# Sums over neighbours by accumulating DMAs in a two-attention kernel on one Trainium2 core

## The chip, the cores and the metric

The kernel runs on one core of one Trainium2 chip. The metric is the device time of one execution in microseconds (us); the time before is the median of three runs. The engines are TensorE (PE), VectorE (DVE), ScalarE (ACT), GpSimd (POOL) and SyncE (SP). In the kernel before, SP starts every DMA.

## What is computed

One sequence of 2048 positions with 512 features goes through two attentions with 32 heads of width 16. A is full attention. B is local: each position looks at itself and at seven earlier ones, two apart. A gate per position mixes the two results.

```python
x = A_x                                              # (1, 2048, 512) bf16
g = _sigmoid((x * gate_w).sum(-1, keepdims=True))
# A: full attention, H = 32, Dh = 16
scores = jnp.einsum("bhqd,bhkd->bhqk", q, k) * (Dh ** -0.5)
o = jnp.einsum("bhqk,bhkd->bhqd", _softmax(scores, axis=-1), v)
a = o.transpose(0, 2, 1, 3).reshape(B, S, D) @ A_wo
# B: local attention, W = 8 neighbours, dil = 2
idx = pos[:, None] - (jnp.arange(W) * dil)[None, :]  # masked where idx < 0
logits = jnp.einsum("bhsd,bhswd->bhsw", q, kg) * scale
o = jnp.einsum("bhsw,bhswd->bhsd", _softmax(logits, axis=-1), vg)
b = o.transpose(0, 2, 1, 3).reshape(B, S, D) @ B_wo
return g * a + (1 - g) * b
```

In both attentions q, k and v are `x @ wqkv`. The change touches the last sum of B, over the eight neighbours w of attn[w] * vg[w].

## The kernel before

**Full attention (A).** The queries are split into four chunks of 512 positions, and the heads into eight groups of four. A chunk with a group is a period; there are 32. In each period the scores of 16 key tiles for four heads are made by PE in two PSUM rings of three and two banks. ACT turns each ring into exponentials (`pT`), 683 such instructions in the whole kernel, and PE multiplies them with v into the one bank `acc`. A part of the exponentials (3 to 12 tiles a period) is made by DVE with integer arithmetic instead: `dt_a` or `wkv` from the bank `D`, then three shifted copies `pd_a`. At the end of a period DVE transposes `acc` (`accT`), POOL scales it by the denominators and the gate (`rden`, `ott`), and DVE transposes every second one into `oat`, which holds the transposed results of one chunk and comes in two buffers (`po3`, L1241).

**Local attention (B).** It runs beside A, 16 tiles of 128 positions (`b_tile`, L799). PE projects k, v and q of the tile into the one PSUM bank `misc_ps`, DVE copies them to `kvs` and `qb`, and SP writes `kvs` to the DRAM scratch `kv_scr`. From there SP loads the shifted keys and values, four neighbours in each of two loads (`ksh`, `vsh`, 512 KB each, in three shared buffers `gat`). The rest is done by POOL in pieces of 128x256:

- the logits: 16 products `prod<-ksh,qb` and their additions into `lg` (about 22 us),
- the softmax: `sm_sub` on POOL after a maximum by DVE, the exponential on ACT, sums and reciprocals on DVE, then the gate (`sm_gate`) and `sm_mul` on POOL,
- the weighted values: 16 products `prod<-vsh,lg` (`av_mul`, L920) and 14 additions (`av_add`, L936), which add neighbours pairwise in `prod` and into `ob`, the last two into the bf16 tile `obb`.

The pieces of logits and values of one tile are strung together by `chain_ops` (L948). The result `obb` is transposed by PE into `misc_ps` (`fin`, L1006) and copied by DVE to `obt`, which holds the four tiles of a chunk and comes in two buffers.

**Output projections.** When a chunk of A is complete (the last `oat` is written) and B's tile is in `obt`, PE multiplies both with the two output weights into one bank, eight matmuls a tile, two at a time (`ab_part`, L1275). DVE copies the sum to `osb` and SP stores it. In the last chunk a part of this is left for the very end.

**The order.** Nothing is ordered by hand. Every step is an `Op` with an engine, an assumed duration, a due time (`dl`), the steps it needs, and tokens for the buffers that it allocates and uses. `list_schedule` (L159) plays these steps on a model of the five engines and writes one fixed order for every engine, into which the program is then emitted. On the chip every engine goes through its list in that order and waits at semaphores. The starts of B's tiles are given: the first at 36, then 44 to 49 apart (`b_space`), each allowed to start its projections 70 earlier. Due times of B's steps are offsets from these starts. The due times of the output projections are offsets from the end of A's chunk, `E`, which is the sum of assumed durations of A (L1273):

```python
dl = E + (4.0 + 4.0 * tt if last else 10.0 + 14.0 * tt)
```

A step on POOL is assumed to last `PRE` plus a price per element by its kind:

```python
NS = dict(bb=0.00189, bf=0.00178, ff=0.00212, one=0.0011)
GP = lambda kind, n: [(False, PRE), (True, NS[kind] * n)]
```

Of the kernel before, what the change touches and what calls it, by code (L numbers as in the profile page):

```python
# [8 lines left out]
ACT = mybir.ActivationFunctionType  # L9
ALU = mybir.AluOpType  # L10
AX = mybir.AxisListType
FP32 = mybir.dt.float32
# [17 lines left out]
W = 8  # L30
# [35 lines left out]
class Op:  # L66

    def __init__(self, eng, occ, fn, dl, deps=(), alloc=(), use=(), lat=None, rel=0.0, name="",
                 mode="f", js=(), full=0.0, fill=False, scores=None, after=(), ride=False, parts=None):
        self.scores, self.ride, self.parts = scores, ride, parts  # L70
# [16 lines left out]
NS = dict(bb=0.00189, bf=0.00178, ff=0.00212, one=0.0011)  # L87
GFIRST = -300.0
PRE = 0.14
GP = lambda kind, n: [(False, PRE), (True, NS[kind] * n)]  # L90
# [68 lines left out]
def list_schedule(ops, zeros):  # L159
# [16 lines left out]
    def avail(o):  # L176
        t = o.ready
        for tk in o.alloc:
            r = tk.res
            n = len(r.order)  # L180
            if n >= r.cap:
                for u in r.order[n - r.cap].ops:
                    if u.done is None:
                        return INF
                    t = max(t, u.end + SELF[u.eng] if u.eng == o.eng else u.done)
        return t
# [15 lines left out]
    while len(out) < len(ops):  # L202
# [54 lines left out]
        for s_ in succ.get(o, ()):  # L257
            left[s_] -= 1
            if left[s_] == 0:
                s_.ready = max([s_.rel] + [d.end + SELF[d.eng] if d.eng == s_.eng else d.done for d in s_.deps] + [d.t for d in s_.after])  # L260
                cand[s_.eng].append(s_)
# [4 lines left out]
def kernel(  # L266
# [156 lines left out]
    kv_scr = tc.dram_tile([16 + S, 2 * D], BF16, name="kv_scr")  # L423
    NH = NG // 2
    woarr = const.tile([128, NH, D], BF16, name="woarr")
    ident = const.tile([128, 128], BF16, name="ident")
    identf = const.tile([128, 128], FP32, name="identf")
    rowc = const.tile([128, 3], FP32, name="rowc")
# [23 lines left out]
    omg = const.tile([128, NT], FP32, name="omg")  # L452
    e1 = const.tile([128, NT], FP32, name="e1")
    d1 = const.tile([128, NT], FP32, name="d1")

# [23 lines left out]
    def init_pool2():  # L479
        make_identity(nc, identf[:])  # L480
        G.memset(vp_all[:, 0, :, :], 1.0)
        G.memset(vp_all[:, 1:NT, :, DH:DH + 1], 1.0)
# [283 lines left out]
    def zsig():  # L766
        A.activation(out=e1[:], in_=st_g["zp"][:, 0:NT], func=ACT.Exp, scale=-1.0)

    def zgate():
        V.tensor_scalar_add(out=d1[:], in0=e1[:], scalar1=1.0)  # L770
        V.reciprocal(out=g_sp[:], in_=d1[:])
        V.tensor_tensor(out=omg[:], in0=e1[:], in1=g_sp[:], op=ALU.mult)

    def zrows():
        st_g["zr"] = misc_ps([128, NT, TPC])
        for s_ in range(TPC):
            for j in range(4):
                mm(st_g["zr"][32 * j:32 * j + 32, :, s_], identf[:, 32 * s_:32 * s_ + 32], g_sp[:], True, True,
                   tile_position=(0, 32 * j))
# [14 lines left out]
    obt_tiles, obt_tok = {}, {}  # L794
    WH = W // 2
    WP = WH // 2
    HB = D // 2

    def b_tile(t):  # L799
# [52 lines left out]
        tks, tvs = [tok("gat", NGA), tok("gat", NGA)], [tok("gat", NGA), tok("gat", NGA)]  # L852
        tlg, tob, tbb = tok("lg", 2), tok("ob", 1), tok("obb", 1)
        kvd_ = o_kvd[max(0, t - 1):t + 1] + [o_zr]
# [3 lines left out]
        def logits_mul(hf, wp, w_, c0):  # L858
            def s():
                if hf == 0 and wp == 0 and w_ == 0 and c0 == 0:  # L860
                    st["lg"] = work.tile([128, H, W], FP32, name="lg", tag="lg", bufs=2)
                if w_ == 0 and c0 == 0:
                    st["prod", hf, wp] = work.tile([128, WP, D], FP32, name="prod", tag="prod", bufs=2)
# [56 lines left out]
        def av_mul(hf, wp, w_, c0):  # L920
            def s():
                if wp == 0 and w_ == 0 and c0 == 0:
                    key = ("ob", "obb")[hf]
                    st[key] = work.tile([128, D], (FP32, BF16)[hf], name=key, tag=key, bufs=1)
                if w_ == 0 and c0 == 0:
                    st["prod", hf, wp] = work.tile([128, WP, D], FP32, name="prod", tag="prod", bufs=2)
# [4 lines left out]
                G.tensor_tensor(out=st["prod", hf, wp][:, w_, c0:c0 + HB].rearrange("p (h d) -> p h d", d=DH),  # L931
                                in0=st["vsh", hf][:, wp + w_, c0:c0 + HB].rearrange("p (h d) -> p h d", d=DH),
                                in1=attn_bc, op=ALU.mult)
            return s, "bf", HB
# [12 lines left out]

        def chain_ops(seq, dls, alloc, toks):  # L948

            made, tps, a, seen = {}, {}, None, set()  # L950
            for n_, (g_, k_, (f, kind, n), src, deps) in enumerate(seq):
                new = g_ not in tps
                if new:
                    tps[g_] = tok("prod", 2)
                al, us = list(alloc.get((g_, k_), ())), []
# [27 lines left out]
        aseq = []  # L983
        loads["k", t], loads["v", t] = lk, lv
# [7 lines left out]
        a = op("pool", 0.0, sm_mul, GFIRST, deps=[a], use=[tlg], parts=GP("ff", H * W))  # L992
        for g_, (hf, wp) in enumerate(halves):
            k1 = range(1 if not hf and not wp else 2)
            ps_ = mulp(av_mul, hf, wp) + [av_add(hf, wp, c0, k_) for k_ in k1 for c0 in range(0, D, HB)]
            srcs = [None] * nm + [2, 3] + [nm, nm + 1]
            gs_ = [(g_, k_, p_, srcs[k_], ([lv[hf], a] if k_ == 0 else [])) for k_, p_ in enumerate(ps_)]
            aseq += [gs_[k_] for k_ in (0, 2, 4, 1, 3, 5, 6, 7) if k_ < len(gs_)]
        a1 = chain_ops(aseq, tb + 40, {(0, 0): [tob], (WH // WP, 0): [tbb]},
                       lambda g_: [tlg, tvs[g_ // (WH // WP)], tob] + ([tbb] if g_ >= WH // WP else []))  # L1000
        a1.lat += SM_LAT[3]
        tk = tok("misc", 1)
        if cb not in obt_tok:
            obt_tok[cb] = tok("obt", 2)

        def fin():  # L1006
            if cb not in obt_tiles:
                obt_tiles[cb] = work.tile([128, DC, QW], BF16, name="obt", tag="obt", bufs=2)
            st["ptp"] = misc_ps([128, DC, 128], BF16)
# [202 lines left out]
    for pi, (c_, i) in enumerate(periods):  # L1212
        st = {}
        if i == 0:
            oat_tok[c_] = tok("oat", 2)
        if i % 2 == 0:
# [24 lines left out]
        def po3(pi=pi, c_=c_, i=i):  # L1241
            if c_ not in oat_tiles:
                oat_tiles[c_] = work.tile([128, NH, QW], BF16, name="oat", tag="oat", bufs=2)
            V.transpose(out=oat_tiles[c_][:, i // 2, :], in_=ott2[:, (pi // 2) % 2].rearrange("p b d -> p (b d)"))
# [21 lines left out]
    for t in range(NT):  # L1266
# [5 lines left out]
        E = S0[NG * c_ + ng]  # L1272
        dl = E + (4.0 + 4.0 * tt if last else 10.0 + 14.0 * tt)  # L1273

# [95 lines left out]
```

## Time and profile before

| | |
|---|---|
| median of three runs | 825.94 us (825.35 to 826.28) |
| profiled execution, its own time | 826.04 us |
| its span in the profile | 824.3 us |
| mean granted TensorE clock | 0.994 |
| DMA | 47.37 MB, 57 GB/s on average |
| DMAs started by POOL | none |

The span runs from the first to the last instruction of the program; the 1.74 us between it and the execution's own time lie around it. Busy time of an engine is the time in which one of its instructions ran; a matmul's end is modelled. In the waits a line reads: engine, what it writes, what it waited for, then the total in us, the number of waits and the longest. In the groups by form a line reads: line of the code, engine, operation, output and inputs with their shapes, the count, then the busy us, the mean ns of one, and the idle time ahead of them. In the timeline a line begins with its start and its length in us, and ends with the idle time of the engine ahead of it and what ended that. L323 and L332 are helpers through which nearly all instructions are issued, so the tiles' names tell them apart. L1011 is `fin`.

### The profile page before, as it was taken

What the parts mean: (1) busy time and instruction counts of PE and PEld (TensorE: products, weight loads), DVE (VectorE), ACT (ScalarE), POOL (GpSimd) and SP (SyncE); (2) the same over time, 40 slices, a digit from 0 to 9 for tenths busy, and PEclk for the clock granted to TensorE, in tenths of its full rate; (3) what the DMA queues carried; (4) which work ended last, traced back from release to release, by engine and by line L of the source; (5) the groups of instructions that cost most, each with busy time, mean ns of one, the idle gap of its engine ahead of it and who ended that gap; (6) DMA issues with size and microseconds to landing.
All of it is one profiled execution on the core that took longest, in us unless ns stands there. A gap on an engine that the chain in (4) does not pass through costs nothing.

```text
span 824.3 us, 18657 instructions
## 1 busy us (share of the span) xinstructions
PE 777.9 (94%) x7314; PEld 247.4 (30%) x7358; DVE 706.3 (86%) x1111; ACT 785.9 (95%) x706; POOL 720.4 (87%) x1196
## 2 busy tenths in 40 slices
PE   7999999999999999999999999999999999999996
PEld 4333433333322222222222222222222222222231
DVE  5456876788978999989999899999989899998987
ACT  3899999999899899999999999999999999999995
POOL 5097999999999999899999999899999999899960
PEclk9899999999999999999999999999999999999999
DMA  9203020112111220211112111211111211110000
GB/s 296 78 3 116 2 90 28 65 52 65 57 48 65 65 66 28 63 53 47 63 35 77 57 50 51 65 53 49 43 52 54 82 34 65 52 52 27 27 1 26
DMA packets 44440, 47.37 MB, mean 57 GB/s; under 512 B 2352, under 2 KB 41776, under 8 KB 44352
## 3 DMA queue, kind: packets, MB, share of 16 engines
q1 hardware_dynamic: 44352, 46.18, 17.6%
q8 instruction: 57, 0.93, 0.5%
q14 instruction: 31, 0.25, 0.1%
HBM read 39.85 MB, written 6.32 MB: 56 GB/s over the span
## 4 chain that ended last, share of the span: by engine, by line
ACT 47%; PE 31%; issue 18%; DVE 2%; DMA 1%; SPq 0%; DVEq 0%; ACTq 0%
ACT pT L323 46%; PE acc L332 11%; PE ring L332 9%; PE misc_ps L332 8%; PE D L332 3%; DMA xld<-in_A_x_dram 1%; ACT lg L323 1%; DVE pd_a L323 0%; DVE kt_all L323 0%; PE pxt L584 0%; PE misc_ps L1011 0%; DVE dt_a L323 0%; DVE qt L323 0%; DVE vp_all L323 0%; DVE wkv L323 0%
## 5 line engine op out<-in xcount | busy, mean ns | idle before, releaser
L323 ACT ACTIVATE pT<-ring 128x1536 bf16<-128x1536 f32 (+1 forms) x684 | 778.8, 1319 | 20.5 <-PE acc L332 14.0
L332 PE MATMUL ring<-qt,kt_all 32*128 32x512 bf16 x1709 | 272.0, 382 | 28.4 <-ACT pT L323 19.2
L323 POOL TENSOR_TENSOR prod<-prod 128x256 f32<-128x256 f32 x352 | 235.6, 677 | 13.2
L332 PE MATMUL acc<-pT,vp_all 128*17 128x512 bf16 (+1 forms) x1709 | 189.0, 385 | 0.3 <-DVE accT L323 0.2
L323 POOL TENSOR_TENSOR prod<-ksh,qb 128x256 f32<-128x256 bf16 x256 | 166.5, 673 | 22.5 <-DMA ksh<-kv_scr 21.7
L323 DVE TENSOR_SCALAR pd_a<-dt_a 128x1536 uint16<-128x1536 uint16 x195 | 180.4, 941 | 1.2
L332 PEld LDWEIGHTS <-kt_all 32*128 32x128 bf16 x2048 | 91.2, 91 | 294.1 <-issue 285.2
L323 DVE TENSOR_SCALAR dt_a<-D 128x512 uint16<-128x512 f32 x195 | 132.7, 680 | 39.2 <-PE D L332 38.5
L323 POOL TENSOR_TENSOR prod<-vsh,lg 128x256 f32<-128x256 bf16 x256 | 162.0, 652 | 0.0
L323 DVE TENSOR_SCALAR pd_a<-wkv 128x1536 uint16<-128x1536 uint16 x144 | 131.0, 945 | 1.9 <-PE acc L332 0.3
L332 PE MATMUL acc<-pd_a,vd_all 128*17 128x512 bf16 x1017 | 130.0, 381 | 0.0
L332 PE MATMUL D<-qt,kt_all 32*128 32x512 bf16 x339 | 128.7, 380 | 1.0 <-DVE kt_all L323 0.4
L323 DVE TENSOR_SCALAR wkv<-D 128x512 uint16<-128x512 f32 x144 | 98.2, 682 | 7.5 <-PE D L332 5.9
L332 PE MATMUL misc_ps<-z 128*32 128x512 bf16 x260 | 85.3, 387 | 1.6 <-DVE z L323 1.6
L332 PEld LDWEIGHTS <-vp_all 128*17 128x17 bf16 (+1 forms) x1709 | 43.7, 88 | 74.9 <-issue 66.6
L332 PEld LDWEIGHTS <-vd_all 128*17 128x17 bf16 x1356 | 42.3, 88 | 64.3 <-issue 51.5
L332 PE MATMUL misc_ps<-bw,xT 128*128 128x512 bf16 x162 | 51.6, 393 | 2.4 <-DVE kt_all L323 0.8
L323 POOL TENSOR_TENSOR ob<-ob,prod 128x256 f32<-128x256 f32 x64 | 45.5, 729 | 0.0
L332 PEld LDWEIGHTS <-z 128*32 128x32 bf16 x341 | 29.9, 96 | 42.2 <-issue 26.1
L332 PEld LDWEIGHTS <-xT 128*128 128x128 bf16 x576 | 30.2, 98 | 36.8 <-issue 31.8
L332 PE MATMUL misc_ps<-xT,wq 128*32 128x512 bf16 x512 | 40.5, 382 | 0.1
L323 DVE TENSOR_SCALAR_CACHE_REDUCE kt_all<-misc_ps,rowc 128x512 bf16<-128x512 f32 x32 | 23.8, 746 | 16.0 <-PE misc_ps L332 15.4
(85 smaller groups left out, 611.9 us busy)
## 6 DMA issues: line engine op xcount, KB each, us to landing
ksh<-kv_scr SPq DMA_DIRECT2D x32, 512.0 KB, 3.9
vsh<-kv_scr SPq DMA_DIRECT2D x32, 512.0 KB, 3.7
kv_scr<-kvs SPq DMA_DIRECT2D x16, 256.0 KB, 2.0
out_dram<-osb SPq DMA_DIRECT2D x16, 128.0 KB, 1.7
xld<-in_A_x_dram SPq DMA_DIRECT2D x3, 512.0 KB, 6.4
bw<-in_B_wqkv_dram SPq DMA_DIRECT2D x1, 1536.0 KB, 11.5
wkv<-in_A_wqkv_dram SPq DMA_DIRECT2D x2, 512.0 KB, 7.3
pd_a<-in_A_x_dram SPq DMA_DIRECT2D x1, 512.0 KB, 8.4
```

Of the source, the lines that this page charges most:

```text
L323: return chain_on(key, f(*a, **k))
L332: return chain(nc.tensor.matmul(out, lhsT=lhsT, rhs=rhs, start=start, stop=stop, **kw))
```

## The change

Of the weighted values of a tile, the products of the first four neighbours are written by POOL straight into a new constant tile `av` (128 x 4 x 512 in fp32). The products of the other four go to two `prod` tiles, and each is added to its half of `av` by an accumulating DMA that POOL starts. A third accumulating DMA adds the upper half of `av` to the lower. POOL then adds the two rows that are left, in two instructions, into `obb`. So 14 POOL additions a tile become three DMAs of 512 KB and two additions. The order's model counts 1.0 us of POOL for each such DMA (`DMAQ`) and 6.0 us from there to its landing (`DMAL`); `far` marks a DMA's end as one that POOL itself has to wait for.

For room in the on-chip memory, `ob` goes away, `obt` and `oat` come in one buffer instead of two, and the fp32 identity and two small tiles of the gate (`identf`, `e1`, `d1`), which are used early, share the room of `av`. `prod` has three buffers instead of two. The due times of the output projections of the first three chunks become earlier and closer together.

```diff
+DMAQ, DMAL = 1.0, 6.0
+NPR = 3
...
-                    t = max(t, u.end + SELF[u.eng] if u.eng == o.eng else u.done)
+                    t = max(t, u.end + SELF[u.eng] if u.eng == o.eng and not u.far else u.done)
...
-    identf = const.tile([128, 128], FP32, name="identf")
+    av = const.tile([128, WH, D], FP32, name="av")
+    identf = av[:, 0, 0:128]
...
-    e1 = const.tile([128, NT], FP32, name="e1")
-    d1 = const.tile([128, NT], FP32, name="d1")
+    e1, d1 = av[:, 1, 0:NT], av[:, 1, NT:2 * NT]
...
         def av_mul(hf, wp, w_, c0):
             def s():
...
+                if hf == 0:
+                    o_ = av[:, wp + w_, c0:c0 + HB]
+                else:
+                    if w_ == 0 and c0 == 0:
+                        st["av", wp] = work.tile([128, WP, D], FP32, name="prod", tag="prod", bufs=NPR)
+                    o_ = st["av", wp][:, w_, c0:c0 + HB]
...
-        def av_add(hf, wp, c0, k_):
-            def s():
-                prod, ob = st["prod", hf, wp], st["ob"]
-                cs = slice(c0, c0 + HB)
-                if not hf and not wp:
-                    G.tensor_tensor(out=ob[:, cs], in0=prod[:, 0, cs], in1=prod[:, 1, cs], op=ALU.add)
-                elif k_ == 0:
-                    G.tensor_tensor(out=prod[:, 0, cs], in0=prod[:, 0, cs], in1=prod[:, 1, cs], op=ALU.add)
...
-                    G.tensor_tensor(out=(st["obb"] if hf and wp else ob)[:, cs], in0=ob[:, cs], in1=prod[:, 0, cs], op=ALU.add)
-            return s, "ff", HB
+        def av_sum(wp):
+            def s():
+                if wp is None:
+                    G.dma_start(out=av[:, 0:WP, :], in_=av[:, WP:WH, :], accum_op=ALU.add)
+                else:
+                    G.dma_start(out=av[:, wp:wp + WP, :], in_=st["av", wp][:], accum_op=ALU.add)
+            return s
+
+        def av_last(c0):
+            def s():
+                if c0 == 0:
+                    st["obb"] = work.tile([128, D], BF16, name="obb", tag="obb", bufs=1)
+                G.tensor_tensor(out=st["obb"][:, c0:c0 + HB], in0=av[:, 0, c0:c0 + HB], in1=av[:, 1, c0:c0 + HB], op=ALU.add)
+            return s
...
+        tav = tok("av", 1)
+        b, sums = None, []
+        for hf, wp in halves:
+            tp_ = tok("prod", NPR) if hf else None
+            for n_, (w_, c0) in enumerate((w_, c0) for w_ in range(WP) for c0 in range(0, D, HB)):
+                al = ([tav] if hf == wp == 0 else [tp_] if hf else []) if n_ == 0 else []
+                us = [x for x in (tav, tp_) if x is not None and x not in al]
+                b = op("pool", 0.0, av_mul(hf, wp, w_, c0), tb + 40, deps=[lv[hf], a], after=[b], alloc=al, use=us + [tlg, tvs[hf]],
+                       name=f"B{t}", parts=GP("bf", HB))
+            if hf:
+                b = op("pool", DMAQ, av_sum(wp), tb + 41, deps=[b], use=[tav, tp_], lat=DMAQ + DMAL, far=True, name=f"B{t}")
+                sums.append(b)
+        a1 = op("pool", DMAQ, av_sum(None), tb + 42, deps=sums, use=[tav], lat=DMAQ + DMAL, far=True, name=f"B{t}")
+        b = op("pool", 0.0, av_last(0), tb + 43, deps=[a1], alloc=[tbb], use=[tav], name=f"B{t}", parts=GP("ff", HB))
+        a1 = op("pool", 0.0, av_last(HB), tb + 43, deps=[a1], after=[b], use=[tav, tbb], name=f"B{t}", parts=GP("ff", HB))
...
-            obt_tok[cb] = tok("obt", 2)
+            obt_tok[cb] = tok("obt", 1)
...
-            oat_tok[c_] = tok("oat", 2)
+            oat_tok[c_] = tok("oat", 1)
...
-        dl = E + (4.0 + 4.0 * tt if last else 10.0 + 14.0 * tt)
+        dl = E + (4.0 + 4.0 * tt if last else 2.0 + 4.0 * tt)
```

More of the change, by code (lines that the diff above doesn't have):

```diff
@@ L68, in __init__ @@
     def __init__(self, eng, occ, fn, dl, deps=(), alloc=(), use=(), lat=None, rel=0.0, name="",
-                 mode="f", js=(), full=0.0, fill=False, scores=None, after=(), ride=False, parts=None):
-        self.scores, self.ride, self.parts = scores, ride, parts
+                 mode="f", js=(), full=0.0, fill=False, scores=None, after=(), ride=False, parts=None,
+                 far=False):
+        self.scores, self.ride, self.parts, self.far = scores, ride, parts, far
         if parts is not None:
@@ L259, in list_schedule @@
             if left[s_] == 0:
-                s_.ready = max([s_.rel] + [d.end + SELF[d.eng] if d.eng == s_.eng else d.done for d in s_.deps] + [d.t for d in s_.after])
+                s_.ready = max([s_.rel] + [d.end + SELF[d.eng] if d.eng == s_.eng and not d.far else d.done for d in s_.deps] + [d.t for d in s_.after])
                 cand[s_.eng].append(s_)
@@ L424 @@
     NH = NG // 2
+    WH = W // 2
     woarr = const.tile([128, NH, D], BF16, name="woarr")
     ident = const.tile([128, 128], BF16, name="ident")
-    identf = const.tile([128, 128], FP32, name="identf")
+    av = const.tile([128, WH, D], FP32, name="av")
+    identf = av[:, 0, 0:128]
     rowc = const.tile([128, 3], FP32, name="rowc")
@@ L479, in init_pool2 @@
     def init_pool2():
-        make_identity(nc, identf[:])
+        make_identity(nc, identf)
         G.memset(vp_all[:, 0, :, :], 1.0)
@@ L766, in zsig @@
     def zsig():
-        A.activation(out=e1[:], in_=st_g["zp"][:, 0:NT], func=ACT.Exp, scale=-1.0)
+        A.activation(out=e1, in_=st_g["zp"][:, 0:NT], func=ACT.Exp, scale=-1.0)
     def zgate():
-        V.tensor_scalar_add(out=d1[:], in0=e1[:], scalar1=1.0)
-        V.reciprocal(out=g_sp[:], in_=d1[:])
-        V.tensor_tensor(out=omg[:], in0=e1[:], in1=g_sp[:], op=ALU.mult)
+        V.tensor_scalar_add(out=d1, in0=e1, scalar1=1.0)
+        V.reciprocal(out=g_sp[:], in_=d1)
+        V.tensor_tensor(out=omg[:], in0=e1, in1=g_sp[:], op=ALU.mult)
     def zrows():
@@ L777, in zrows @@
             for j in range(4):
-                mm(st_g["zr"][32 * j:32 * j + 32, :, s_], identf[:, 32 * s_:32 * s_ + 32], g_sp[:], True, True,
+                mm(st_g["zr"][32 * j:32 * j + 32, :, s_], av[:, 0, 32 * s_:32 * s_ + 32], g_sp[:], True, True,
                    tile_position=(0, 32 * j))
@@ L794 @@
     obt_tiles, obt_tok = {}, {}
-    WH = W // 2
     WP = WH // 2
@@ L852, in b_tile @@
         tks, tvs = [tok("gat", NGA), tok("gat", NGA)], [tok("gat", NGA), tok("gat", NGA)]
-        tlg, tob, tbb = tok("lg", 2), tok("ob", 1), tok("obb", 1)
+        tlg, tbb = tok("lg", 2), tok("obb", 1)
         kvd_ = o_kvd[max(0, t - 1):t + 1] + [o_zr]
@@ L862, in s @@
                 if w_ == 0 and c0 == 0:
-                    st["prod", hf, wp] = work.tile([128, WP, D], FP32, name="prod", tag="prod", bufs=2)
+                    st["prod", hf, wp] = work.tile([128, WP, D], FP32, name="prod", tag="prod", bufs=NPR)
                 G.tensor_tensor(out=st["prod", hf, wp][:, w_, c0:c0 + HB], in0=st["ksh", hf][:, wp + w_, c0:c0 + HB],
@@ L921, in s @@
             def s():
[L922 to L926, printed above, removed]
+                if hf == 0:
[4 more added lines that the diff above has]
+                    o_ = st["av", wp][:, w_, c0:c0 + HB]
                 attn = st["lg"]
@@ L930, in s @@
                 attn_bc = _ap(a0, [list(a0.ap[0]), [W, hn], [0, DH]])
-                G.tensor_tensor(out=st["prod", hf, wp][:, w_, c0:c0 + HB].rearrange("p (h d) -> p h d", d=DH),
+                G.tensor_tensor(out=o_.rearrange("p (h d) -> p h d", d=DH),
                                 in0=st["vsh", hf][:, wp + w_, c0:c0 + HB].rearrange("p (h d) -> p h d", d=DH),
                                 in1=attn_bc, op=ALU.mult)
-            return s, "bf", HB
-        def av_add(hf, wp, c0, k_):
+            return s
+        def av_sum(wp):
             def s():
-                prod, ob = st["prod", hf, wp], st["ob"]
-                cs = slice(c0, c0 + HB)
-                if not hf and not wp:
-                    G.tensor_tensor(out=ob[:, cs], in0=prod[:, 0, cs], in1=prod[:, 1, cs], op=ALU.add)
-                elif k_ == 0:
-                    G.tensor_tensor(out=prod[:, 0, cs], in0=prod[:, 0, cs], in1=prod[:, 1, cs], op=ALU.add)
-                else:
-                    G.tensor_tensor(out=(st["obb"] if hf and wp else ob)[:, cs], in0=ob[:, cs], in1=prod[:, 0, cs], op=ALU.add)
-            return s, "ff", HB
+                if wp is None:
+                    G.dma_start(out=av[:, 0:WP, :], in_=av[:, WP:WH, :], accum_op=ALU.add)
+                else:
+                    G.dma_start(out=av[:, wp:wp + WP, :], in_=st["av", wp][:], accum_op=ALU.add)
[5 more added lines that the diff above has]
+                G.tensor_tensor(out=st["obb"][:, c0:c0 + HB], in0=av[:, 0, c0:c0 + HB], in1=av[:, 1, c0:c0 + HB], op=ALU.add)
+            return s
         def chain_ops(seq, dls, alloc, toks):
@@ L953, in chain_ops @@
                 if new:
-                    tps[g_] = tok("prod", 2)
+                    tps[g_] = tok("prod", NPR)
                 al, us = list(alloc.get((g_, k_), ())), []
@@ L982, in b_tile @@
             lseq += ad[:3] + nxt[:2] + ad[3:] + nxt[2:]
-        aseq = []
         loads["k", t], loads["v", t] = lk, lv
@@ L992, in b_tile @@
         a = op("pool", 0.0, sm_mul, GFIRST, deps=[a], use=[tlg], parts=GP("ff", H * W))
[L993 to L1000, printed above, removed]
+        tav = tok("av", 1)
[13 more added lines that the diff above has]
+        a1 = op("pool", 0.0, av_last(HB), tb + 43, deps=[a1], after=[b], use=[tav, tbb], name=f"B{t}", parts=GP("ff", HB))
         a1.lat += SM_LAT[3]
@@ L1003, in b_tile @@
         if cb not in obt_tok:
-            obt_tok[cb] = tok("obt", 2)
+            obt_tok[cb] = tok("obt", 1)
         def fin():
             if cb not in obt_tiles:
-                obt_tiles[cb] = work.tile([128, DC, QW], BF16, name="obt", tag="obt", bufs=2)
+                obt_tiles[cb] = work.tile([128, DC, QW], BF16, name="obt", tag="obt", bufs=1)
             st["ptp"] = misc_ps([128, DC, 128], BF16)
@@ L1242, in po3 @@
             if c_ not in oat_tiles:
-                oat_tiles[c_] = work.tile([128, NH, QW], BF16, name="oat", tag="oat", bufs=2)
+                oat_tiles[c_] = work.tile([128, NH, QW], BF16, name="oat", tag="oat", bufs=1)
             V.transpose(out=oat_tiles[c_][:, i // 2, :], in_=ott2[:, (pi // 2) % 2].rearrange("p b d -> p (b d)"))
```

## The prediction

> **What bounds the kernel now.** I read the page first: busy times, then the chain.
>
> ```profile
> span 824.3 us, 18657 instructions
> PE 777.9 (94%) x7314; PEld 247.4 (30%) x7358; DVE 706.3 (86%) x1111; ACT 785.9 (95%) x706; POOL 720.4 (87%) x1196
> ACT 47%; PE 31%; issue 18%; DVE 2%; DMA 1%; SPq 0%; DVEq 0%; ACTq 0%
> ```
>
> ScalarE (ACT) and TensorE (PE) carry the chain; GpSimd (POOL), the engine that the change relieves, is not in it. The waits say what stops ACT, and what stops POOL:
>
> ```profile
> ACT pT L323 <- PE acc L332: 14.0, 9, 3.1
> POOL lg L323 <- DVE mx L323: 10.2, 14, 2.3
> POOL rr L323 <- DVE rr L323: 4.9, 10, 0.9
> PEld L1011 <- POOL prod L323: 1.8, 6, 0.4
> ```
>
> Nobody loses time to POOL: PE waits 1.8 us for the local attention's sums, ACT never. ACT's idle time is 38.4 us. The timeline puts 14.0 of it ahead of its first exponential at 19.67, 3.6 between 26 and 33, 8.8 behind its last (815.49). About 12 lies between, mostly in these places (start, length, operation, idle time before):
>
> ```profile
> 206.44 1.45 ACT L323 ACTIVATE pT<-ring 128x1536 bf16<-128x1536 f32 x1 [1.90 <-PE acc L332]
> 209.94 31.76 ACT L323 ACTIVATE pT<-ring 128x1024 bf16<-128x1024 f32 x28 [2.04 <-PE acc L332]
> 273.66 15.97 ACT L323 ACTIVATE pT<-ring 128x1024 bf16<-128x1024 f32 x14 [2.16 <-PE acc L332]
> 636.76 3.72 ACT L323 ACTIVATE pT<-ring 128x1536 bf16<-128x1536 f32 x3 [1.09 <-PE acc L332]
> 787.73 13.66 ACT L323 ACTIVATE pT<-ring 128x1024 bf16<-128x1024 f32 x12 [1.24 <-PE acc L332]
> ```
>
> The last three, with 0.32 at 463 and 0.28 at 471, lie in the four stretches in which PE makes the output projections (248 to 278, 440 to 467, 633 to 662, 773 to 801): 5.1 us. The others at 94 (1.72), 156 (0.47), 204 and 208 (together 6.1) lie where projections of both attentions crowd PE. So the change can win at most these 11 us.
>
> **POOL's tile.** By form, operation by operation (count, busy us, mean ns):
>
> ```profile
> L323 POOL TENSOR_TENSOR prod<-vsh,lg 128x256 f32<-128x256 bf16 x256 | 162.0, 652 | 0.0
> L323 POOL TENSOR_TENSOR ob<-ob,prod 128x256 f32<-128x256 f32 x64 | 45.5, 729 | 0.0
> L323 POOL TENSOR_TENSOR ob<-prod 128x256 f32<-128x256 f32 x32 | 23.2, 726 | 2.2
> L323 POOL TENSOR_TENSOR obb<-ob,prod 128x256 bf16<-128x256 f32 x32 | 22.8, 732 | 0.0
> ```
>
> A tile's 14 additions are 4 + 2 + 2 of these and 6 of the 128x256 `prod<-prod` (0.735 us). Back to back two take 1.37 to 1.41 in the timeline, so 0.69 each. Removed: 14; added: 2 of the last form. Saved: 12 x 0.69 = 8.3 us a tile. The local attention's exponentials start from 68.07 (tile 0) to 757.39 (tile 15), 45.95 apart, and POOL has hardly a pause: its tile falls to 37.7 us and three DMA issues.
>
> **The issue.** No DMA is issued by POOL in this trace. The nearest rows are SP's:
>
> ```profile
>   L323 SPq DMA_DIRECT2D ksh<-kv_scr x32: 359/360/1434, 35.0 to 715.9; - x32
> ksh<-kv_scr SPq DMA_DIRECT2D x32, 512.0 KB, 3.9
> ```
>
> One issue holds SP 0.36 us, at most 1.43. Lower bound 0.36; upper 1.43 plus one of VectorE's (DVE's) 0.94 us operations in its way, 2.4. I take 1.2, nearer the long SP issues, as the DMA also waits for POOL's own last product. Three make 3.6: a tile of 41.3, 4.6 less than now. The written order counts 1.0 each (`DMAQ`), so the chip would fall 0.6 a tile behind the order; POOL's waits for DVE's maximum (10.2 / 16 = 0.64 a tile) shrink by as much, since DVE's queue is then already there. Left: nothing, with 0.5 us allowed.
>
> **The landing.** 512 KB read and written lands 3.9 us after the issue. An accumulation reads its target too: between 3.9 and, twice over, 7.8. The order waits 7 (`DMAQ` + `DMAL`). I take 6: hidden. Behind the third DMA's wait, and behind the last addition's, stands the next tiles' logits work on POOL (about 22 us of it a tile), then `sm_sub`, for which ACT's exponential waits, and `obb`, for which PE's `fin` waits. The order fills both flights with logits, so a landing by 7 costs nothing; every microsecond beyond costs one, twice a tile. The DMA engines are 10 to 20% busy in most slices, so 24 MB read twice and written once fit; a gather that overlaps one may land some us later, and its order has 7 us against 3.9.
>
> **Earlier tiles.** At 41.3 a tile the last tile's sums come at about 796.5 - 15 x 4.6 = 727. Nothing ends then: ACT still has its 683 large exponentials (901 us by their rows, which overlap). So 4.6 x 16 = 74 us of POOL buy no end time by themselves. They move PE's work: tile 15's `fin` and projection leave the stretch around 786, and a little more projection work falls into 60 to 210. That second part: between 2 us less and 2 more of the 6.1; I take +0.5.
>
> **Output projections.** New due times put four tiles 4 us apart where they lay 7 to 14 apart: 32 matmuls of about 0.22 us a slot, 7 us of PE in 16. The 5.1 us that they cost now (0.6 in the cheapest full stretch, 2.16 in the dearest) can go to 0 or to 4 x 2.16 = 8.6. With tiles 3, 11 and 15 no longer late I take 0.9 a stretch, 3.6: -1.5.
>
> **Single buffers.** `oat` is first written for the next chunk at 297.3, 488.7 and 677.9, 15 us and more after the last projection of the old one: nothing. `obt`: the next chunk's first `fin` comes at 310, 497 and 687; with a faster POOL tile 12's sums, now at 682.9, would be ready near 682.9 - 12 x 4.6 = 628, and its `fin` must wait for projections that end near 650. `obb` is held till then, and POOL needs it again for tile 13's, near 670: nothing. The shared constants (`identf`, `e1`, `d1`) are read by 55, before POOL's first product into `av` (95): nothing.
>
> **Sum.** 826.04 (the profiled execution: span 824.3 and 1.74 around it; 0.1 above the median of 825.94) - 1.5 + 0.5 + 0.5 = 825.5 us.
>
> **Rivals.**
> *POOL falls behind its order (slower).* All queues are in one fixed order, so a POOL that needs more than the order counts holds `sm_sub` and `obb`, and ACT and PE stand. It decides from 1.2 us an issue: beyond that 3 x (X - 1.2) a tile are lost until the order itself lets POOL rest. Tiles may start their projections 70 us ahead of their nominal start; from 32 behind at tile 0, gaining 3 to 8 a tile, that is about ten tiles. At X = 2.0: 2.4 x 10 - 1 (median lead of `sm_sub` over its exponential, 0.9) = 23: 849; at 2.4: 861; at 1.5: 834. For it: ACT's lead is only 0.08 to 1.5 us, so a slip shows at once. Against: DVE seems not to hold POOL up:
>
> ```profile
>   L323 POOL TENSOR_TENSOR prod<-ksh,qb x256: 657/669/1125, 39.3 to 749.1; 128x256 f32<-128x256 bf16 x128
>   L323 DVE TENSOR_SCALAR pd_a<-dt_a x195: 892/943/957, 38.5 to 805.5; 128x1536 uint16<-128x1536 uint16 x195
>   L323 DVE TENSOR_SCALAR pd_a<-wkv x144: 895/944/956, 259.2 to 813.3; 128x1536 uint16<-128x1536 uint16 x144
> ```
>
> DVE's shifts run 339 x 0.943 = 320 us, 39% of the span; were POOL shut out by them, its median product (0.669) could not lie within 0.012 of its fastest. The Trainium skill, SBUF — State Buffer, section SBUF: two separate sides, speaks against this change: it says that a DMA issued from GpSimd has its descriptors written by GpSimd, which a VectorE instruction in a two-port mode locks out. By that rule every issue that meets a shift would be up to 0.94 us longer and this rival would be the forecast; the rows above show the shifts locking out no GpSimd arithmetic, and no run here shows an issue. Chance 0.25.
> *All projection gaps go (faster).* 826.04 - 5.1 - 0.5 = 820.4. For it: three of the five gaps follow late `fin`s (265.9, 638.2, 778.1); against: the dearest also meets the change of the accumulator at 270.6. Chance 0.20.
> *The dense projections stall PE (slower).* 826.04 + 3.5 + 1 = 830.5. Against: the 440 to 467 stretch cost 0.6. Chance 0.10.
> *POOL isn't relieved.* Landings take the 4.6 back as waits and no more: 826. It lies inside the forecast's case.
>
> **Numbers.** Forecast's case 0.45, its own range 822.5 to 828.5; in it faster 0.15, same 0.17, slower 0.13. 0.2% of 825.94, 1.7 us, is about what a measurement of this kernel can tell. Faster 0.15 + 0.20 = 0.35; same 0.17; slower 0.13 + 0.25 + 0.10 = 0.48. The range reaches down past 820.4 to 819 and up to an issue of 1.9, 845.
>
> **What would show it.** Right: POOL's busy time near 720 - 16 x 8.3 = 587, its last sum before 740, no wait of ACT's `lg` or PE's `obb` on POOL or a DMA above 5 us in all, ACT busy unchanged (786), gaps beside the projections summing to 3 to 4. The issue rows give X and the landing against 1.2 and 6. Wrong: POOL waiting for `av` DMAs, or ACT's `lg` for POOL, by tens of us; an ACT end far from 815; or new ACT gaps where each chunk ends (247, 438, 630).

## The result and the profile after

The kernel after takes 837.66 us (median of 4 runs, 835.95 to 838.85) against 825.74 for the kernel before beside it: ratio 1.0142, interval 1.0123 to 1.0161. The change costs 11.9 us. The profiled execution took 838.85 us, span 837.0.

The head of its page, and the shares of the chain:

```profile
span 837.0 us, 18618 instructions
...
PE 788.6 (94%) x7347; PEld 253.4 (30%) x7388; DVE 708.7 (85%) x1111; ACT 787.2 (94%) x706; POOL 627.0 (75%) x1052
...
ACT 42%; PE 31%; issue 16%; POOL 6%; DVE 2%; DMA 2%; SPq 0%; DVEq 0%; ACTq 0%; POOLq 0%
```

POOL was relieved as far as forecast (720.4 to 627.0, of which 42.4 are the new issues), and has entered the chain all the same, with 6%. ACT has the work that it had (787.2 against 785.9), but stands idle for 837.0 - 787.2 = 49.8 us, where it was 38.4. These 11.4 us and the 1.3 of busy time are the whole difference of the spans. The waits name those who make them (total, count, longest):

```profile
POOL av L326 <- DMA av<-prod: 28.9, 13, 4.7
...
ACT pT L326 <- PE acc L335: 17.7, 11, 3.1
...
ACT pT L326 <- PE ring L335: 11.6, 11, 5.2
...
POOL obb L326 <- DMA av<-av: 5.7, 2, 3.8
...
PEld L1024 <- POOL obb L326: 2.5, 2, 1.6
PE misc_ps L1024 <- POOL obb L326: 2.1, 2, 1.5
...
ACT lg L326 <- POOL lg L326: 1.6, 2, 1.2
```

ACT's waits for `acc` and for the rings were 14.0 and 5.7 before (now 17.7 and 11.6); the other five lines are new. The wait for the rings in the kernel before:

```profile
ACT pT L323 <- PE ring L332: 5.7, 2, 5.2
```

The timeline of ACT puts the gaps in two kinds of place. The first is beside the output projections:

```profile
257.12 12.32 ACT L326 ACTIVATE pT<-ring 128x1024 bf16<-128x1024 f32 x11 [1.62 <-PE acc L335]
271.48 5.97 ACT L326 ACTIVATE pT<-ring 128x1536 bf16<-128x1536 f32 x5 [2.04 <-PE acc L335]
...
454.24 7.01 ACT L326 ACTIVATE pT<-ring 128x1536 bf16<-128x1536 f32 x6 [2.39 <-PE acc L335]
...
650.92 13.88 ACT L326 ACTIVATE pT<-ring 128x1024 bf16<-128x1024 f32 x12 [2.13 <-PE acc L335]
...
792.38 15.93 ACT L326 ACTIVATE pT<-ring 128x1536 bf16<-128x1536 f32 x14 [2.05 <-PE acc L335]
```

With 0.45 at 461 and 0.31 at 789 this makes 11.0 us; it was 5.1. The second kind is where POOL comes late. One such place, POOL first, then PE, then ACT:

```profile
494.55 0.87 POOL L326 DMA_DIRECT2D av<-av  x1 [0.92 <-DMA av<-prod]
501.76 2.54 POOL L326 TENSOR_TENSOR prod<-ksh,qb 128x256 f32<-128x256 bf16 x4 [6.34 <-DMA ksh<-kv_scr]
504.27 1.39 POOL L326 TENSOR_TENSOR prod<-prod 128x256 f32<-128x256 f32 x2
505.63 0.71 POOL L326 TENSOR_TENSOR obb<-av 128x256 bf16<-128x256 f32 x1
...
507.37 0.72 POOL L326 TENSOR_TENSOR obb<-av 128x256 bf16<-128x256 f32 x1
```

```profile
508.15 0.28 PE L1024 MATMUL misc_ps<-ident,obb 128*128 128x128 bf16 x2 [1.46 <-POOL obb L326]
```

```profile
508.90 2.37 ACT L326 ACTIVATE pT<-ring 128x1536 bf16<-128x1536 f32 x2 [1.28 <-PE ring L335]
```

The third DMA is started, then POOL's list holds the next tile's products, whose load of `ksh` lands only at 501.7. The additions into `obb` stand behind them in the list; `fin` on PE stands behind those, and the scores for ACT's ring behind `fin`. With 0.86 and 0.36 that follow at 511 and 516, ACT loses 2.5 us here. At 146.5 it loses 1.22 to a late `sm_sub`. The load at 501.7 is not late through POOL alone: the write of `kvs` ahead of it, issued at 490.71, took 5.3 us to land (2.0 in the median before), and the load, issued at 496.11 beside the third accumulation and two more loads, 5.5 (3.9 before).

The new DMAs themselves, in the DMA part of the trace and in the tile's own rows (min, median, max of the issue in ns):

```profile
ksh<-kv_scr SPq DMA_DIRECT2D x32, 512.0 KB, 4.8
vsh<-kv_scr SPq DMA_DIRECT2D x32, 512.0 KB, 4.3
av<-prod POOLq DMA_DIRECT2D x32, 512.0 KB, 5.1
av<-av POOLq DMA_DIRECT2D x16, 512.0 KB, 5.2
```

```profile
L326 POOL DMA_DIRECT2D av<-prod x32: 862/878/1052, 104.7 to 774.0; - x32
L326 POOL DMA_DIRECT2D av<-av x16: 858/876/896, 119.2 to 779.0; - x16
```

An issue is 0.88 us, and 0.30 more of waiting for POOL's own last product ahead of 30 of the 32 into `av<-prod`. The landing, counted from the start of the issue, is 5.1 in the median, 4.5 at best; but 10.2 and 9.8 in tiles 0 and 8, where loads of `ksh` and `vsh` fly at the same time. Of the 48 landings 12 take longer than the 7 us that the order counts.

### The profile page after: what moved, and what is told of

Read it like the earlier page. It is cut to its first block, busy times and chain, and to the rows that moved or that the text cites. A ratio compares the mean times of both kernels' runs of the same rounds, so it can differ in the third digit from the quotient of the medians.

```text
span 837.0 us, 18618 instructions
## 1 busy us (share of the span) xinstructions
PE 788.6 (94%) x7347; PEld 253.4 (30%) x7388; DVE 708.7 (85%) x1111; ACT 787.2 (94%) x706; POOL 627.0 (75%) x1052
## 2 busy tenths in 40 slices
DMA packets 51351, 72.53 MB, mean 87 GB/s; under 512 B 3120, under 2 KB 42544, under 8 KB 51264
## 4 chain that ended last, share of the span: by engine, by line
ACT 42%; PE 31%; issue 16%; POOL 6%; DVE 2%; DMA 2%; SPq 0%; DVEq 0%; ACTq 0%; POOLq 0%
ACT pT L326 42%; PE acc L335 11%; PE ring L335 9%; PE misc_ps L335 8%; POOL prod L326 4%; PE D L335 3%; DMA av<-prod 1%; POOL av L326 1%; DMA xld<-in_A_x_dram 1%; DVE dt_a L326 0%; POOL lg L326 0%; ACT lg L326 0%; POOL obb L326 0%; PE pxt L588 0%; DVE kt_all L326 0%
## 5 line engine op out<-in xcount | busy, mean ns | idle before, releaser
L326 ACT ACTIVATE pT<-ring 128x1536 bf16<-128x1536 f32 (+1 forms) x684 | 779.1, 1327 | 30.3 <-PE acc L335 17.7
L326 POOL TENSOR_TENSOR prod<-ksh,qb 128x256 f32<-128x256 bf16 x256 | 170.5, 705 | 57.7 <-DVE pd_a L326 21.7
L335 PE MATMUL acc<-pT,vp_all 128*17 128x512 bf16 (+1 forms) x1709 | 192.3, 386 | 0.3 <-DVE accT L326 0.3
L326 POOL TENSOR_TENSOR prod<-prod 128x256 f32<-128x256 f32 (+1 forms) x256 | 170.2, 682 | 5.8
L335 PE MATMUL misc_ps<-z 128*32 128x512 bf16 x285 | 94.5, 387 | 1.8 <-DVE z L326 1.6
L326 POOL TENSOR_TENSOR prod<-vsh,lg 128x256 f32<-128x256 bf16 x128 | 84.0, 753 | 0.0
L326 POOL TENSOR_TENSOR av<-vsh,lg 128x256 f32<-128x256 bf16 x128 | 78.4, 645 | 0.1
L335 PEld LDWEIGHTS <-z 128*32 128x32 bf16 x371 | 32.8, 96 | 43.3 <-issue 25.3
```

What stands on the lines that cost most here:

```text
L326: return chain_on(key, f(*a, **k))
L335: return chain(nc.tensor.matmul(out, lhsT=lhsT, rhs=rhs, start=start, stop=stop, **kw))
```

## Experiments

Two suspects stood at the start: the dense due times (D), and an order written with too short an issue and landing (P). Later a third appeared in the traces: VectorE (DVE) instructions held up beside POOL's products. Ratios are against the kernel before, run on the same chip beside them.

### The due times alone, each way

`x2_before_new_due`: the kernel before with the new due times and nothing else.

```diff
-        dl = E + (4.0 + 4.0 * tt if last else 10.0 + 14.0 * tt)
+        dl = E + (4.0 + 4.0 * tt if last else 2.0 + 4.0 * tt)
```

> The kernel before with only the new due times of the output projections; two buffers each for obt and oat, POOL additions, no accumulating DMA. Theory D: slower by about 7, 831 to 834. Theory P and theory M: as before, 825 to 827.

Measured: 832.21 us, ratio 1.0080 (1.0065 to 1.0095), so 6.5 us for this line alone. ACT's timeline of this kernel, beside the output projections:

```profile
255.96 11.42 ACT L323 ACTIVATE pT<-ring 128x1536 bf16<-128x1536 f32 x10 [1.66 <-PE acc L332]
269.42 13.66 ACT L323 ACTIVATE pT<-ring 128x1536 bf16<-128x1536 f32 x12 [2.04 <-PE acc L332]
...
448.31 5.54 ACT L323 ACTIVATE pT<-ring 128x1024 bf16<-128x1024 f32 x5 [1.73 <-PE acc L332]
454.93 15.93 ACT L323 ACTIVATE pT<-ring 128x1536 bf16<-128x1536 f32 x14 [1.08 <-PE acc L332]
```

With 1.01, 1.18 and 1.10 in the third stretch and 1.51 in the fourth: 11.3 us, against 5.1. That is 6.2 of the 6.5. No DMA of POOL's is in this kernel. What PE does ahead of the gap that ends at 448.31:

```profile
445.36 1.04 PE L332 MATMUL misc_ps<-bwo,obt 128*128 128x512 bf16 x4
446.23 0.59 PE L332 MATMUL misc_ps<-woarr,oat 128*128 128x512 bf16 x2
...
446.76 0.60 PE L332 MATMUL ring<-qt,kt_all 32*128 32x512 bf16 x3
447.30 0.60 PE L332 MATMUL misc_ps<-woarr,oat 128*128 128x512 bf16 x2
447.83 0.39 PE L332 MATMUL acc<-pT,vp_all 128*17 128x512 bf16 x4
```

The eight projection matmuls of a tile run from 445.36 to 447.90. ACT's next scores (`ring`) are there at 447.36, but it has no free buffer for its result: `pT` comes in three buffers a ring, and one becomes free only when PE has multiplied it into `acc`. These multiplications stand behind the projections, and ACT starts at 448.31.

`x1_old_due`: the kernel after with the line undone.

> The changed kernel with the due times of the output projections of the kernel before (10 + 14 a tile instead of 2 + 4); all else as changed. Theory D (dense output projections): some 7 of the change's 12 us come from the denser projections, since the ACT exponentials fall back by 1.8, 3.0, 1.6 and 1.0 us in the four projection stretches: 829 to 833. Theory P (POOL late: its accumulating DMAs land later than the written order allows): the projections do not matter: 836 to 839. Theory M (earlier B tiles crowd PE everywhere): 835 to 838.

Measured: 838.86 us, ratio 1.0159 (1.0143 to 1.0174). No gain: the gaps beside the projections fall to 7.0 us, and as much comes up elsewhere. P's number held, and the two causes do not add up.

### The order's allowances

`x4_old_due_l9`: x1 with 1.2 us counted for an issue and 9 for a landing. The chip's work is the same; only the order on the engines differs.

```diff
-DMAQ, DMAL = 1.0, 6.0
+DMAQ, DMAL = 1.2, 9.0
```

> The changed kernel with the due times of before, and with an order written for 1.2 us an issue and 9 us from there to the landing (instead of 1.0 and 6.0). Theories D and P together: both losses go, 824 to 828. D alone: as the run with only the old due times, 829 to 833. M: 835 to 838.

Measured: 825.98 us, ratio 1.0002 (0.9993 to 1.0011): 12.9 us less than x1, and the time of the kernel before. Its page's busy times and the first of its waits that matter:

```profile
PE 786.4 (95%) x7353; PEld 248.4 (30%) x7353; DVE 705.7 (86%) x1111; ACT 786.8 (95%) x706; POOL 627.1 (76%) x1052
```

```profile
POOL av L326 <- DMA av<-prod: 19.1, 5, 5.2
...
ACT pT L326 <- PE acc L335: 9.9, 9, 3.1
```

POOL still waits for DMAs, but no wait of ACT or PE on POOL's `lg` or `obb` is left. ACT's gaps beside the projections are 3.1 us; its idle time in all is 823.9 - 786.8 = 37.1.

`z4_issue12` counts 1.2 and 6, `z3_landing9` 1.0 and 9, both with the old due times.

> The changed kernel with the old due times and 1.2 us an issue, the landing left at 6.0. If the landing is what the order had too short: 834 to 839. If the issue: 826 to 830.

> The changed kernel with the old due times and 9 us to the landing, the issue left at 1.0. If the landing is what the order had too short: 826 to 830. If the issue: 835 to 839.

Measured: 832.24 (ratio 1.0075, 1.0060 to 1.0090) and 830.98 (1.0087, 1.0053 to 1.0122; its five times spread from 830.70 to 837.60, with a mean of 833.3). Neither fell into a range that was expected. By the medians each takes half of the loss away or a little more (by its mean, z3 takes 5.5 us); only both together took it all. In z4 ACT still waits 2.8 us for `lg`. In z3's trace a masking by DVE is held 3.04 us at 407, as in x1 (see below), so what is left there need not all be the allowance for the issue.

`z2_l9_new_due`: 1.2 and 9, with the change's dense due times.

> The changed kernel (new, dense due times) with an order written for 1.2 us an issue and 9 us to the landing. If the dense projections cost the same 6.5 us as in the kernel before: 831 to 834. If they cost only where POOL is late too: 826 to 829.

Measured: 834.81 (1.0105, 1.0090 to 1.0121), just above the first range and 8.8 above x4. The gaps beside the projections are 10.8 us. Another gap of 2.78 lies at 562, behind a masking by DVE that is held 2.87 us, so the 8.8 are not the projections alone.

| median, us | old due times | dense due times |
|---|---|---|
| kernel before | 825.7 | 832.2 |
| after, counting 1.0 and 6 | 838.9 (x1) | 837.7 (the change) |
| after, counting 1.0 and 9 | 831.0 (z3) | |
| after, counting 1.2 and 6 | 832.2 (z4) | |
| after, counting 1.2 and 9 | 826.0 (x4) | 834.8 (z2) |

### Shorter transfers

`x3_short_dma`: the change, with each accumulating DMA over 32 of the 512 columns.

```diff
-                    G.dma_start(out=av[:, 0:WP, :], in_=av[:, WP:WH, :], accum_op=ALU.add)
+                    G.dma_start(out=av[:, 0:WP, 0:32], in_=av[:, WP:WH, 0:32], accum_op=ALU.add)
...
-                    G.dma_start(out=av[:, wp:wp + WP, :], in_=st["av", wp][:], accum_op=ALU.add)
+                    G.dma_start(out=av[:, wp:wp + WP, 0:32], in_=st["av", wp][:, :, 0:32], accum_op=ALU.add)
```

> The changed kernel, every engine's order of instructions unchanged, but each accumulating DMA adds only 32 of the 512 columns (32 KB instead of 512 KB), so the sums of the other columns are left out. Landings fall from 4.5-10 us to about 2-3. Theory P: the POOL waits for av go and ACT wins 4 to 6 us: 831 to 834. Theory D and theory M: 836 to 838.

Measured: 836.64 (1.0134, 1.0117 to 1.0151), only 1.0 us less than the change, and outside P's range. The DMAs land in 2.8 to 3.0 us in the median, the loads of `ksh` and `vsh` in 4.0 and 3.8 again, and the two losses at 146 and 507 are gone; but an issue takes 1.20 us (the shape is another), and one new hole of 5.1 us opens in ACT's work at 199. DVE's timeline there:

```profile
194.58 4.69 DVE L326 TENSOR_TENSOR vd_all<-vp_all,wts 128x1632 bf16<-128x1632 bf16 x1
```

In the kernel before the same form takes 2.08 at most. It lasts this long while POOL runs an issue, four products and an issue without a pause. So the run did not separate landing from issue as meant, but it showed the third suspect.

### Single buffers

`z1_single`: the kernel before with one buffer each for `obt` and `oat`.

> The kernel before with obt and oat in one buffer each, nothing else; every engine's list of instructions stays the same. If single buffers cost nothing at POOL's old pace: 825 to 827. If they cost waits: 828 or more.

Measured: 826.01, ratio 0.9999 (0.9990 to 1.0009). Nothing, at POOL's old pace.

### DVE held beside POOL's products

In x1 ACT's exponentials fall 3.85 us further behind around 410. All 32 maskings of x1 (min, median, max in ns), then DVE and POOL at this place:

```profile
L326 DVE TENSOR_SCALAR qt<-qt,qmask x32: 340/497/3386, 18.1 to 776.8; 128x256 uint32<-128x256 uint32 x32
```

```profile
407.36 3.39 DVE L326 TENSOR_SCALAR qt<-qt,qmask 128x256 uint32<-128x256 uint32 x1
410.67 0.68 DVE L326 TENSOR_SCALAR wkv<-D 128x512 uint16<-128x512 f32 x1
```

```profile
405.81 0.87 POOL L326 DMA_DIRECT2D av<-prod  x1 [0.30 <-POOL prod L326]
406.42 2.83 POOL L326 TENSOR_TENSOR prod<-ksh,qb 128x256 f32<-128x256 bf16 x4
408.93 2.45 POOL L326 TENSOR_TENSOR prod<-prod 128x256 f32<-128x256 f32 x3
```

```profile
411.40 0.38 PE L335 MATMUL acc<-wkv,vd_all 128*17 128x512 bf16 x1 [1.52 <-DVE wkv L326]
```

The masking of `qt`, 0.50 us in the median, lasts 3.39, while POOL's instructions follow each other so closely that their records overlap; it ends at 410.74, just behind the only pause, 0.08 us between the second and the third `prod<-prod`. DVE's next result is late, and PE waits for it.

The traces show that it is POOL that holds it. In the traces of all runs together 27 maskings last over 1.2 us, and every one ends 0.16 us (0.32 in y4, below) behind the end of a POOL instruction, 22 of them where POOL pauses. A run of POOL instructions is not enough for a hold: the maskings of x1 at 72.53, 437.24 and 523.78 meet runs of 1.2 to 3.4 us and last 0.72 to 0.81, each ending 0.15 us behind the end of the first POOL instruction. The two kinds differ in POOL's rows: beside these three, neighbouring instructions overlap by 0.04 us, beside the 27 by 0.26 to 0.34. Why POOL overlaps them more at some places was not found.

Three kernels change only the masking's form, in the order of x1: 16-bit elements (y1), a constant in place of the mask (y3), every second element (y4), and a fourth reads and writes in pieces of unlike shape (y5).

```diff
-            u = qt_tiles[pi][:].bitcast(U32)
-            V.tensor_scalar(out=u, in0=u, scalar1=qmask[:, 0:1], ...)
+            u = qt_tiles[pi][:].bitcast(U16)                                    # y1, y3
+            V.tensor_scalar(out=u, in0=u, scalar1=qmask[:].bitcast(U16)[:, 0:1], ...)   # y1, y4; y3 with scalar1=0x7FFF
+            u = qt_tiles[pi][:].bitcast(U16).rearrange("p (n two) -> p two n", two=2)      # y4
+            u = qt_tiles[pi][:].bitcast(U16)[:, 0:511]           # y5, in0=u.rearrange("p (a b) -> p a b", a=7)
```

> The kernel after with the old due times (838.86 before), and DVE's masking of `qt` read as 128x512 uint16 in place of 128x256 uint32. All else, every engine's order too, is that kernel's. There one masking was held 3.39 us at 407.36 behind an unbroken run of POOL products (median 0.50), and ACT's exponentials slipped 3.85 us around it. Theory H (the form of the masking decides whether POOL can hold it: DVE's 339 uint16 shifts never took more than 0.96): no masking over 1.0 us, and the 3.85 us largely gone: 834 to 836. Theory S (POOL's run holds any DVE instruction that starts beside it there, or the instruction's own semaphore wait is what the record shows): a masking of over 2 us again, 838 to 840. Theory N (the held masking is a symptom, and the slip has another cause): no masking over 1.0 us, yet 838 to 840.

> The kernel of y1_mask16 with a constant (0x7FFF) in place of the mask `qmask` that DVE reads per partition from the on-chip memory; the order on every engine is the same. It masks all rows, also those that the kernel leaves as they are, so the scores are others. The rows so far: DVE's shifts (one input and a constant) never took over 0.96 us, also beside the POOL products of 402 to 409, while the masking (input and mask) was held 3.38 us there, in both widths. Theory O (an instruction that reads a second operand from the memory is held until POOL's run lets go): no masking over 1.0 us, PE's wait for DVE's `wkv` near 411 gone, and 2 to 4 us less than y1's 837.54: 833.5 to 835.5. Theory I (any instruction at this place is held, by its own semaphore or by POOL): a masking of over 2 us, 836.5 to 838.5. Theory N (the masking is free but the time is lost elsewhere): no masking over 1.0 us and 836.5 to 838.5.

> The kernel of y1_mask16 (837.54) with the masking reading and writing every second 16-bit element, 128x2x256, in place of neighbouring ones; the mask is read as there, the order on every engine is the same. In the fastest cases so far a masking of 512 elements takes 0.28 to 0.34 us, so it moves more than one element in a nanosecond; the shifts, which were never held, move 1536 in 0.94. Theory P (what is held is an instruction that works at the fast rate of two or more ports, or reads two tiles; the POOL products that follow each other without a gap keep it out until POOL pauses): with the stride the masking runs at the slow rate, 0.5 to 0.8 us, none over 1.0, PE's wait for `wkv` near 411 is gone, 834 to 836. Theory I (any DVE instruction between on-chip tiles at this place is held): over 2 us again, 836.5 to 838.5.

> The kernel after with the old due times (838.86), the masking of `qt` over 511 of the 512 columns, read as 7 pieces of 73 and written as one of 511; it leaves one column unmasked, so its scores are others. The order on every engine is the same. So far 512 neighbouring 16-bit elements took 0.28 to 0.34 us at least and every second one 0.50, both held 3.4 to 3.6 us near 407, while the shifts, which are read and written in unlike pieces, are at 1.6 elements a nanosecond and were never held. Theory P (only the fast rates, which the unlike pieces rule out, are held by POOL): 0.4 to 0.8 us, none over 1.0, PE's wait for `wkv` near 411 gone; 834 to 836. Theory I (any DVE instruction from on-chip tile to on-chip tile at this place is held): over 2 us again, 837 to 839.

Measured: 837.54, 837.39, 837.29 and 837.14 us (ratios 1.0147, 1.0137, 1.0132 and 1.0143, each with about 0.0018 to either side). The hold was there in all: at most 3.38, 3.39, 3.56 and 3.40 us, at the same place. So neither the width nor the second operand decides. y4 needs 0.32 us behind POOL's end where the others need 0.16; that is 512 elements at 1.6 a nanosecond (an estimate from these rows), the rate of the shifts, and it was held all the same, so the fast rate is not needed for a hold. y5 at its fastest took 0.34, like y1: its seven pieces lie side by side, and nothing shows that DVE read them as seven.

`y6_no_mask` is x1 without the masking; `y7_l9_no_mask` is x4 without it.

> The kernel after with the old due times, without the masking: it leaves the sign bits in all rows of `qt`, so its scores are others; the other instructions keep their order. If the held masking is what costs the 2.4 to 3.9 us near 407 (H): they are gone, as are parts of the 1.1 to 2.5 near 561 (held 1.7 to 2.5 there): 833 to 835. If the slip there comes from POOL's lateness alone (N): 836 to 838.

> The control for y6: the kernel after with the old due times, 1.2 us an issue and 9 us a landing (825.98), without the masking. There no masking took over 0.94 us, so what goes is 32 instructions of about 0.42 us on DVE, an engine off the chain: if those cost nothing (H and N alike), 825 to 826.5. If DVE's room itself is worth time: 822 to 824.5, and y6's gain has to be read less this.

Measured: 834.17 (1.0110, 1.0092 to 1.0128) and 826.19 (1.0007, 0.9998 to 1.0016). Leaving the masking out gives nothing where it is not held. Where it is, it gives 3.0 us against y5, run beside it (their single times overlap), and 4.7 against x1, run earlier (4.0 by the ratios). So of the 12.9 us between x1 and x4 about a quarter to a third is DVE held by POOL, and 8.0, the distance of y6 from y7, is left for the other effects of the short allowances, POOL being late behind its order among them; that part was not taken apart further. Theory H's range (833 to 835) held.

### Can the room on POOL be used?

`y2_closer_tiles`: the kernel after counting 1.2 and 9.5, projections due at 12 + 14 a tile, tiles closer together.

```diff
-    b_space=(44.0,) * 4 + (47.0,) * 4 + (49.0,) * 8,
+    b_space=(42.0,) * 4 + (44.0,) * 4 + (46.0,) * 8,
```

> The kernel after with an order that counts 1.2 us an issue and 9.5 us a landing, the output projections due at 12 + 14 a tile, and the local tiles 42, 44 and 46 us apart in place of 44, 47 and 49, so that the 4.6 us that POOL saves a tile are used to start tiles earlier. Theory A (ACT bounds, relief of POOL buys nothing): 825 to 828, like the 825.98 of the same kernel with the old spacing. Theory R (room of POOL can be turned into time if the tiles' projections leave the end of the kernel): 821 to 824. Theory S (closer tiles crowd PE's projections and POOL's order again): 829 to 834.

Measured: 827.21, ratio 1.0017 (1.0008 to 1.0026). Theory A, for this one spacing. No version beat the kernel before.

## Why the prediction was wrong, step by step

The forecast of 825.5 us was 12.2 too low. Its frame held: ACT and PE bound the kernel, and relief of POOL by itself bought nothing. x4 has this relief (93 us of POOL's busy time gone) and takes the time of before; y2 tries to use it and gains nothing. Three steps failed.

**Output projections: the term that failed most.** I took -1.5; the dense due times cost 6.5 alone (x2), and in the change itself the gaps went from 5.1 to 11.0 us. Even my upper end of 8.6, four stretches with one gap of 2.16 each, was too low, since most stretches have two gaps or more. I had counted PE's share of a stretch, 7 us in 16, and found room. But all gaps of x2 and all but one of the change are ended by `acc`: PE makes projection matmuls (all eight of a tile at 448 in x2) ahead of the multiplications that free ACT's buffers, and ACT stands until these are made. The gain that I expected from "tiles 3, 11 and 15 no longer late" did not come either: tile 11's `fin` was early, at 607, and its stretch cost 2.13 instead of 1.09, while those of tiles 3 and 15 stayed at 267 and 801 (266 and 798 before). One of the three gaps from which I had read this, at 636.76, ends ahead of the `fin` at 638.2 that it was said to follow. The dearest gap, I wrote, "also meets the change of the accumulator"; four of the change's five large gaps lie more than 8 us from any such change, so that is not the cause. The rival "the dense projections stall PE", 830.5 at a chance of 0.10, was this mechanism, sized +3.5 against 5.9 to 6.5.

**"Left: nothing, with 0.5 us allowed": the slip behind the order.** The issue itself came out: 0.88 + 0.30 = 1.18 against 1.2 for two of a tile's three, 0.88 for the third. It was a choice between 0.36 and 2.4, with the right reason for a part of it (the wait for POOL's own product) and luck for the rest. But I set the 0.6 us a tile against POOL's waits for DVE's maximum, and let the rival decide "from 1.2 us an issue". It decides earlier: counting 1.2 instead of 1.0 took 6.6 us off x1 (z4); no masking of z4 lasts over 1.43 us, so a part of this may be the hold. The waits that I spent did shrink, from 10.2 to 4.6, but they are not in front of the instruction that is late at 507, which stands behind a load.

**Landing.** 6 us was above the median (5.1), but 7.8 was no bound: 9 to 10 happened beside gathers. I wrote that a gather that overlaps one "has 7 us against 3.9"; the gathers went to 4.8 and 4.3 in the median, and the accumulations doubled. Counting 9 took 7.9 us off x1 by the medians (z3). "Every microsecond beyond costs one" was not shown: in x4 POOL still waits 19.1 us for these DMAs, and no wait of ACT or PE for `lg` or `obb` stands behind it.

**What I had not seen at all** is the hold of DVE. I asked whether DVE shuts out POOL, and its 339 shifts did not; POOL shutting out DVE was not asked. The fear taken from the Trainium skill, SBUF — State Buffer, section SBUF: two separate sides (that issues wait for DVE) did not come true: the issues took 0.86 to 1.05 us beside as many shifts, of which no run shows whether they are in a two-port mode. The Trainium skill, SBUF — State Buffer, section Who interferes with whom, says that a DVE instruction with two SBUF inputs, or in a mode that uses both of its ports, contends with GpSimd, and that whoever comes first keeps the shared ports for its whole instruction. `vd_all` with its two inputs fits that, and so does the length of x1's maskings at 72.53, 437.24 and 523.78, which end 0.15 us behind one POOL instruction. The long hold does not: the masking at 407 lasted over parts of six, which overlap each other.

**Other points.** Gaps beside the projections: 3 to 4 forecast, 11.0 found. Gaps between 60 and 240: +0.5 forecast, +1.8 found (6.1 to 7.9), of which 1.6 are waits for `sm_sub`. ACT's idle time ahead of its first exponential: 14.3 by the timeline, not 14.0, which changes nothing. Last sum before 740: 785.7 found (796.5 before), because the exponentials of the later tiles keep their places on ACT, 5.6 to 28.9 us behind their `sm_sub`, so POOL's room became idle time. POOL busy 587: 627.0, since I had left the 42.4 us of issues out; without them 585 by subtraction, 593 by the other instructions' rows, which overlap them. ACT's busy time 786: 787.2. Single buffers nothing: shown (z1, and x4 has them too). Waits of `lg` and `obb` under 5 us in all: 6.2, small beside the 11.4 of ACT's new idle time; those at 507 reach ACT by way of PE's rings.

How the 11.9 us of the change divide exactly between the dense due times and the short allowances stays open, as the table does not add up: 5.9 us more of gaps lie beside the projections, and the other 5.5 of ACT's new idle time elsewhere, of which the 2.5 near 507 and the 1.2 at 146 were traced to POOL's list, the first of them behind a late load as well.

## What to carry to other kernels

In a kernel whose engines run fixed lists, a new asynchronous step is priced first by what the list assumes of it: here the same instructions took 839 or 826 us by two constants. The pair that lost nothing covers the worst landing of the trace (1.2 + 9 us against 10.2); the pair that lost 12.9 covers only the median (1.0 + 6 against 5.1). When an edit touches two things at once, a due time and a mechanism, run each alone: the line that looked like tidying cost 6.5 us. Relief of an engine that no one waits for bought nothing here, and that engine's work can hold a neighbour. And an engine's share of a stretch does not tell whether there is room in it: look at what its next instructions free, and for whom.

## What the runs showed of the hardware

An accumulating DMA of 512 KB between tiles on the chip, started by GpSimd, keeps that engine 0.86 to 1.05 us and lands, from the start of the issue, 4.5 us later at best, 5.1 in the median, up to 10.2 beside loads of 512 KB; over 32 of 512 columns, two short rows a partition, the issue is longer (1.12 to 1.46 us) and the landing 2.8 to 3.0 in the median, 7.5 at most. Beside the long accumulations the median landing of these loads went from 3.9 and 3.7 us to 4.8 and 4.3, beside the short ones to 4.0 and 3.8.

A DVE instruction of 0.5 us was held 3.4 us beside a run of GpSimd instructions without a pause, in five forms, and one with two inputs took 4.69; the shifts (0.94 us) and all reads from PSUM beside the same runs were not. Where the GpSimd instructions overlapped by about 0.04 us, it got in behind the first of them; where they overlapped by 0.26 to 0.34, it was held over several. What sets the masking apart from the shifts was not found.
